# Splitting the first K load by partitions and the wq load by rows in a one-core decode kernel

## The chip, the cores and the metric

The kernel runs on one core of a Trainium2 chip. The metric is device time in microseconds (us); the time before is the median of three runs, 121.58 us (121.34 to 121.73). One further execution was taken with the hardware profiler; every profile line comes from that one. Its own time and its span are in the table further down.

The engines are named as in the profile: PE (matrix multiply), DVE (vector), ACT (scalar activations), POOL, and SP, which computes nothing here and issues nearly all DMA transfers. DMA work is done by 16 DMA engines that serve this core.

## The reference

Eight sequences each decode one token. A layer norm feeds two branches. Branch A is grouped-query attention over the last 1024 positions of a K/V cache; branch B is a gated feed-forward network. The result is the input plus A times silu of B.

```python
B, Sq, D = 8, 1, 512
Hq, Hkv, Sk, Dh = 32, 8, 4096, 128
W = min(4096, max(256, Sk // 4))                 # 1024
q = (x @ wq)                                     # wq: 512 x 4096
k = k_cache[:, :, Sk - W:, :]                    # 8 x 8 x 1024 x 128, bf16
v = v_cache[:, :, Sk - W:, :]
p = softmax(einsum(q, k) * Dh ** -0.5)
A = einsum(p, v) @ wo                            # wo: 4096 x 512
Bf = (gelu(x @ w_gate) * (x @ w_up)) @ w_down    # 512 x 1792, 512 x 1792, 1792 x 512
x = A_x; xn = layernorm(x)
return x + A(xn) * silu(Bf(xn))
```

Everything is bf16. The K and V windows are 16 MB each (8 sequences of 2 MB); wq and wo are 4 MB each; the three feed-forward matrices are 1.75 MB each.

## The kernel before

The program is written for one core, with the order of every engine's work fixed by the source (a manual schedule). Synchronisation is generated: each transfer from SP or ACT takes the next of eight DMA semaphores in turn, numbered 0 to 7, and a transfer also waits until the one that had the same semaphore before it, eight transfers earlier, has landed.

Loading. All big tiles live in a ring of eight slots of 128 partitions by 16 KB (`slot`, L62). `load_cache` (L69) loads one sequence's K or V as two transfers (g = 0 and 1), each of four heads: 128 partitions by 8 KB, 1 MB. On the DRAM side a transfer is 32 groups of positions by 4 heads, with 8 KB contiguous each; group p and head n go to partition 4p + n. The loads are issued by SP in this order: K of sequence 0 (L88), wq in two transfers of 2 MB (L93; 16 KB per partition, contiguous), K of sequence 1, V of sequence 0; then, inside the loop over sequences (L398), K two sequences ahead and V one ahead; then the feed-forward weights (L422, L425), and wo (L436), whose last megabyte goes in three pieces of 640, 256 and 128 KB. The token input x (8 partitions by 1 KB) is issued by ACT (L67) and has semaphore 0; the first K transfer has semaphore 1.

Computing. DVE turns each half K tile with one 32x32-block transpose (`turn_k`, L232). PE computes q from xn and wq, 32 matmuls of 512 columns, k outermost (L245 to L253), so that the first 8 need the first quarter of wq. For each sequence: scores (`scores`, L280), softmax (L303), turning of the probabilities (L326), values (L333), and a gather of the output (L354). At the end the two branches are finished, the last matmuls use the last wo piece (L498), and two DVE operations (L506, L508) make the output, which SP stores (L510).

The end of the program. After the store, SP waits on the eight DMA semaphores and the engines' own semaphores with one waiting instruction after another, in this order: semaphore 2; 3 and 1; 4 and 0; 5 and DVE's; 6 and PE's; 7 and ACT's; then POOL's. Then comes a barrier over all engines. Before the change the store is the 45th transfer, and has semaphore 4.

Of the kernel before, what the change touches and what calls it, by code (L numbers as in the profile page):

```python
# [21 lines left out]
def kernel(  # L22
# [13 lines left out]
    nc = tc.nc  # L36

    B, Sq, D = A_x.shape
    Hkv, Sk, Dh = A_k_cache.shape[1], A_k_cache.shape[2], A_k_cache.shape[3]
# [3 lines left out]
    win0 = Sk - W  # L43
    F = B_w_gate.shape[1]
    inv = float(Dh) ** -0.5
    P = nc.NUM_PARTITIONS
    NK = D // P
    HG = 4
    NG = Hkv // HG
    C = W * HG // P  # L50
# [11 lines left out]
    def slot(name):  # L62
        return ring.tile([P, 2 * ROW], BF16, name=name, tag="slot")
# [2 lines left out]
    x_sb = keep.tile([B, D], BF16, name="x_sb")  # L66
    nc.scalar.dma_start(out=x_sb, in_=A_x.flatten_outer_dims())  # L67

    def load_cache(cache, b, name):  # L69
        t = slot(name).rearrange("p (g x) -> p g x", g=NG)  # L70
        for g in range(NG):
            nc.sync.dma_start(  # L72
                out=t[:, g],
                in_=cache[b, g * HG : (g + 1) * HG, win0:Sk, :].rearrange(
                    "n (p c) d -> p n (c d)", c=C
                ),
            )
        return t

    k_sb, v_sb = {}, {}  # L80

    def load_k(b):
        k_sb[b] = load_cache(A_k_cache, b, "k_sb")

    def load_v(b):
        v_sb[b] = load_cache(A_v_cache, b, "v_sb")

    load_k(0)  # L88
    wq_v = A_wq.rearrange("(p k) n -> p k n", k=NK)
    wq_sb = []  # L90
    for i in range(2):
        t = slot("wq_sb").rearrange("p (k n) -> p k n", k=NK // 2)
        nc.sync.dma_start(out=t, in_=wq_v[:, i * (NK // 2) : (i + 1) * (NK // 2), :])  # L93
        wq_sb += [t[:, k, :] for k in range(NK // 2)]
    load_k(1)
    load_v(0)

# [4 lines left out]
        out=ident,  # L102
        in_=ident,
# [13 lines left out]
        out=xpad,  # L117
        in_=xpad,
# [17 lines left out]
        out=xhat,  # L136
# [9 lines left out]
    with tc.tile_pool(name="ps_x", bufs=1, space=PSUM) as ps_x:  # L146
# [26 lines left out]
        out=hv,  # L173
        in_=hv,
# [7 lines left out]
        out=neg_st,  # L182
        in_=neg_st,
# [8 lines left out]
        out=neg_mv,  # L192
        in_=neg_mv,
# [12 lines left out]
    for g in range(NG):  # L206
        nc.vector.tensor_reduce(
            out=sel[:, g, g * qd : (g + 1) * qd],
            in_=ident.rearrange("p (t g h) -> p g h t", t=4, g=NG)[:, g],
# [5 lines left out]
        out=own, in_=ident.rearrange("p (i e) -> p e i", e=8), axis=AX.X, op=ALU.add  # L215
    )
    pick = consts.tile([P, 4 * NU], BF16, name="pick")
    with nc.allow_low_precision(reason="sums of zeros and a single one"):
        nc.vector.tensor_reduce(
            out=pick, in_=ident.rearrange("p (a e) -> p a e", e=8), axis=AX.X, op=ALU.add  # L220
# [177 lines left out]
    for b in range(B):  # L398
        if b + 2 < B:
            load_k(b + 2)  # L400
        if b + 1 < B:
            load_v(b + 1)
            turn_k(b + 1, 0)
        softmax(b)
        if b + 1 < B:
            scores(b + 1, 0)
        if b >= 1:
            gather(b - 1)
        if b + 1 < B:
            turn_k(b + 1, 1)  # L410
            scores(b + 1, 1)
        turn_p(b)
        values(b)
        keep_o(b)
        if b == 4:
            regroup(0)
# [10 lines left out]
    for u in range(NU):  # L427
        if u % 2 == 0:
            pair = slot("wo_sb").rearrange("p (v j d) -> p v j d", v=2, d=D)
        t = pair[:, u % 2]  # L430
        src = A_wo[u * 1024 : (u + 1) * 1024, :].rearrange("(p j) d -> p j d", j=8)
# [14 lines left out]
    for n, ws in (("z_ps", wgu[0]), ("u_ps", wgu[1])):  # L446
# [15 lines left out]
        out=z2, in0=z2, scalar1=0.044715, scalar2=1.0, op0=ALU.mult, op1=ALU.add  # L462
# [11 lines left out]
        out=hT.rearrange("p j b -> p (j b)"), in_=h_bf.rearrange("p (y j) -> p j y", j=NJ)  # L474
    )
    f_ps = ps_f.tile([P, DT], FP32, name="f_ps")
    for j in range(NJ):
# [11 lines left out]
        out=g_sb, in0=g_sb, scalar1=0.5, scalar2=0.5, op0=ALU.mult, op1=ALU.add  # L489
# [5 lines left out]
    for u in range(NU):  # L495
# [15 lines left out]
        out=out_f.rearrange("b (t d) -> t b d", t=4), in_=out_sb[0 : P : RB, :]  # L511
# [31 lines left out]
```

## Time and profile before

| what | before |
|---|---|
| median of 3 runs | 121.58 us |
| profiled execution, own time | 121.8 us |
| its span | 119.7 us |
| bytes read | 47.46 MB |
| PE, DVE, ACT busy | 74.1, 75.8, 31.4 us |
| DMA mean over the span | 398 GB/s |
| first K transfer: issued, landed after | 0.81 us, 5.4 us |
| store issued | 116.84 us |

The profiled execution's own time is 2.1 us more than its span: that part lies around the span and no view shows it. The page gives the span in 40 slices of about 3 us, with the busy share of the DMA engines in tenths and the GB/s that they moved. A window table gives the same for stretches of any length: the engines' busy times, the granted clock of PE, the share of the 16 DMA engines and the GB/s. A share of 1.00 means that all sixteen were busy throughout. Records that straddle an edge of a window can make a share slightly over 1.

### The profile page before, as it was taken

The numbers are of one execution on the slowest core, as the hardware profiler recorded it, in microseconds if no ns is written. First come the engines' busy times: TensorE is split into PE (matmuls) and PEld (weight loads), VectorE is DVE, ScalarE is ACT, GpSimd is POOL, SyncE is SP. The second block draws the span as 40 slices with busy tenths as digits, with TensorE's granted clock in tenths as the row PEclk, the third lists the DMA queues.
The fourth block names the chain that finished last, engine by engine and source line by source line (L and its number), as shares of the span: only waits on it lengthen the run. The fifth ranks groups of instructions, "written<-read, shape, count | busy, mean of one in ns | idle before, by whom it ended". The sixth has DMA issues, their size and how long they took to land.

```text
span 119.7 us, 2300 instructions
## 1 busy us (share of the span) xinstructions
PE 74.1 (62%) x992; PEld 38.7 (32%) x992; DVE 75.8 (63%) x101; ACT 31.4 (26%) x75; POOL 3.2 (3%) x10
## 2 busy tenths in 40 slices
PE   0100499811994988969687684992994547535460
PEld 0100133300341544535443351450353433134340
DVE  3698820499739999999859959909943232651010
ACT  4600000676007151441612510700616110200000
POOL 2150000000000000000000000000000000000000
PEclk9999999985599999999999998599589755555555
DMA  2999999999999999999999999999999999999930
GB/s 66 394 457 433 411 416 427 430 433 422 427 427 433 419 419 427 435 411 430 430 433 405 430 430 430 411 430 435 424 419 447 422 451 412 434 403 430 402 118 3
DMA packets 6254, 47.61 MB, mean 398 GB/s; under 512 B 732, under 2 KB 868, under 8 KB 1124
## 3 DMA queue, kind: packets, MB, share of 16 engines
q1 hardware_dynamic: 6228, 47.46, 94.5%
q8 instruction: 8, 0.13, 0.4%
q10 hardware_dynamic: 16, 0.01, 0.0%
q14 instruction: 2, 0.02, 0.0%
HBM read 47.46 MB, written 0.01 MB: 397 GB/s over the span
## 4 chain that ended last, share of the span: by engine, by line
DMA 63%; PE 16%; DVE 14%; issue 2%; ACT 2%; SPq 1%; DVEq 0%
DMA wo_sb<-in_A_wo_dram 20%; DMA k_sb<-in_A_k_cache_dram 17%; DMA v_sb<-in_A_v_cache_dram 16%; DMA wq_sb<-in_A_wq_dram 9%; PE q_ps L247 8%; PE S_ps L295 6%; DVE kT L234 5%; DVE qbd L269 2%; DVE mx L305 2%; DVE q_both L260 1%; ACT P_sb L317 1%; PE s_ps L498 1%; DVE q_both L257 1%; SPq L72 1%; PE O_ps L339 1%
## 5 line engine op out<-in xcount | busy, mean ns | idle before, releaser
L295 PE MATMUL S_ps<-kT,qbd 128*128 128x512 bf16 x128 | 34.4, 416 | 14.9 <-DVE kT L234 11.5
L234 DVE STREAM_TRANSPOSE kT<-k_sb 128x2048 int32<-128x2048 int32 x16 | 36.5, 2289 | 4.6 <-DMA k_sb<-in_A_k_cache_dram 4.6
L295 PEld LDWEIGHTS <-qbd 128*128 128x128 bf16 x128 | 12.9, 103 | 32.4 <-issue 17.0
L247 PE MATMUL q_ps<-wq_sb,xnR 128*128 128x512 bf16 x32 | 9.8, 482 | 8.8 <-DMA wq_sb<-in_A_wq_dram 8.8
L315 ACT ACTIVATE nb<-m 32x1 f32<-32x1 f32 x32 | 6.4, 201 | 22.7 <-DVE m L312 22.4
L305 DVE TENSOR_REDUCE mx<-S_ps 128x1 f32<-128x1024 f32 x8 | 9.6, 1195 | 4.1 <-PE S_ps L295 4.1
L317 ACT ACTIVATE P_sb<-S_ps,nb 128x1024 bf16<-128x1024 f32 x8 | 11.1, 1391 | 0.3
L339 PE MATMUL O_ps<-v_sb,pT 128*32 128x128 bf16 x512 | 9.3, 228 | 2.6 <-DVE pT L328 2.6
L339 PEld LDWEIGHTS <-pT 128*32 128x32 bf16 x512 | 7.8, 101 | 5.6 <-issue 3.0
L352 ACT COPY O_sb<-O_ps 128x256 f32<-128x256 f32 x8 | 3.0, 372 | 23.5 <-PE O_ps L339 23.5
L247 PEld LDWEIGHTS <-xnR 128*128 128x128 bf16 x32 | 3.7, 118 | 14.6 <-issue 12.6
L328 DVE STREAM_TRANSPOSE pT<-P_sb 128x512 int32<-128x512 int32 x8 | 5.7, 711 | 3.4 <-ACT P_sb L317 2.8
L257 ACT CAST q_both<-q_ps 128x512 bf16<-128x512 f32 x6 | 3.0, 613 | 16.7 <-PE q_ps L247 16.7
L360 PE MATMUL o_ps<-O_sb,sel 128*32 128x128 f32 x32 | 6.1, 325 | 0.9 <-ACT O_sb L352 0.9
L498 PE MATMUL s_ps<-wo_sb,oT 128*32 128x128 bf16 x128 | 4.4, 307 | 3.4 <-DMA wo_sb<-in_A_wo_dram 3.3
L284 PE MATMUL S_ps<-neg_mv,neg_st 128*128 128x512 bf16 x16 | 4.8, 381 | 1.9 <-DVE q_both L257 1.9
L257 DVE CAST q_both<-q_ps 128x512 bf16<-128x512 f32 x2 | 1.3, 672 | 6.9 <-ACT q_both L257 6.9
L360 PEld LDWEIGHTS o_ps<-O_sb,sel 128*32 128x32 f32 x32 | 3.4, 128 | 5.0 <-issue 1.7
L498 PEld LDWEIGHTS <-oT 128*32 128x32 bf16 x128 | 3.5, 136 | 4.4 <-issue 4.2
L506 DVE TENSOR_TENSOR y<-s_ps,g_sb 128x128 f32<-128x128 f32 x1 | 0.3, 290 | 6.9 <-PE s_ps L498 6.9
L239 DVE MEMSET qbd<- 128x4096 uint32 x1 | 3.5, 3472 | 0.8 <-issue 0.8
L479 PE MATMUL f_ps<-wd_sb,hT 128*32 128x128 bf16 x56 | 1.7, 311 | 3.2 <-DVE hT L473 3.2
(64 smaller groups left out, 48.9 us busy)
## 6 DMA issues: line engine op xcount, KB each, us to landing
k_sb<-in_A_k_cache_dram SPq DMA_DIRECT2D x16, 1024.0 KB, 19.9
v_sb<-in_A_v_cache_dram SPq DMA_DIRECT2D x16, 1024.0 KB, 19.6
wq_sb<-in_A_wq_dram SPq DMA_DIRECT2D x2, 2048.0 KB, 11.3
wo_sb<-in_A_wo_dram SPq DMA_DIRECT2D x3, 1024.0 KB, 25.0
wgu_sb<-in_B_w_gate_dram SPq DMA_DIRECT2D x1, 1792.0 KB, 21.3
wgu_sb<-in_B_w_up_dram SPq DMA_DIRECT2D x1, 1792.0 KB
wd_sb<-in_B_w_down_dram SPq DMA_DIRECT2D x1, 1792.0 KB, 24.9
wo_sb<-in_A_wo_dram SPq DMA_DIRECT2D x1, 640.0 KB, 24.1
```

The source lines that it names most:

```text
L234: nc.vector.transpose(out=t.bitcast(I32), in_=k_sb[b][:, g].bitcast(I32))
L247: nc.tensor.matmul(q_ps[i], xnR[:, k, :, :].rearrange("p j b -> p (j b)"), wq_sb[k][:, i * 512 : (i + 1) * 512], start=(k == 0), stop=(k = ...
L257: e(out=q_bf[:, i * 512 : (i + 1) * 512], in_=q_ps[i])
L284: nc.tensor.matmul(S[b][:, half, :], neg_st.rearrange("p j h -> p (j h)"), neg_mv.rearrange("p a n -> p (a n)"), start=True, stop=False,)
L295: nc.tensor.matmul(S[b][:, half, :], qbd[:, m, b, w, g, :], kv[:, half * 16 : (half + 1) * 16, m, :, w], start=False, stop=(g == NG - 1 an ...
L305: nc.vector.tensor_reduce(out=mx, in_=S[b].rearrange("p a c -> p (a c)"), axis=AX.X, op=ALU.max)
L315: nc.scalar.mul(nb[32 * j : 32 * j + 32, :], m1, -inv)
L317: nc.scalar.activation(out=P_sb[b].rearrange("p c i w -> p c w i"), in_=S[b].rearrange("p a (c w i) -> p (a c) w i", w=2, i=32), func=ACT.Exp,
L328: nc.vector.transpose(out=pT[b].rearrange("p c h w -> p (c h w)").bitcast(I32), in_=P_sb[b].rearrange("p c i w -> p (c i w)").bitcast(I32),)
L339: nc.tensor.matmul(O_ps[b][32 * t : 32 * t + 32, g, :], pT[b][:, c // 2, :, c % 2], vv[:, c, :], start=(c < 4), stop=(c >= C - 4),)
L360: nc.tensor.matmul(o[:, 0:Dh], sel[:, g, :], O_sb[b][:, g, :], start=(g == 0), stop=(g == NG - 1))
L498: nc.tensor.matmul(s_ps[32 * t : 32 * t + 32, :], oT[:, j, u, :], wo[u][:, j, t * DT : (t + 1) * DT], start=(u == 0 and j == 0), stop=(u = ...
```

## The change

The first transfer (K of sequence 0, g = 0) becomes two of 64 partitions each: partitions 0 to 63, then 64 to 127. Each takes 16 of the 32 position groups, with 4 heads each; rows stay 8 KB. wq becomes four transfers of 1 MB, one for each k: 128 rows of 8 KB, which lie 32 KB apart in DRAM. The order of everything else stays. Three transfers are added, so all later transfers move on by three in the turn of the eight semaphores; x keeps semaphore 0, the halves have 1 and 2, K's second transfer 3, wq 4 to 7, and the store is the 48th and has semaphore 7. DVE's first transpose waits for both halves, and each group of eight q matmuls for its own wq transfer. No other engine's instructions change.

```diff
-    def load_cache(cache, b, name):
+    def load_cache(cache, b, name, parts=None):
         t = slot(name).rearrange("p (g x) -> p g x", g=NG)
         for g in range(NG):
-            nc.sync.dma_start(
-                out=t[:, g],
-                in_=cache[b, g * HG : (g + 1) * HG, win0:Sk, :].rearrange(
-                    "n (p c) d -> p n (c d)", c=C
-                ),
+            src = cache[b, g * HG : (g + 1) * HG, win0:Sk, :].rearrange(
+                "n (p c) d -> p n (c d)", c=C
             )
+            if parts is not None and g == 0:
+                parts(t[:, g], src)
+            else:
+                nc.sync.dma_start(out=t[:, g], in_=src)
         return t
 
     k_sb, v_sb = {}, {}
 
+    def first_load(dst, src):
+        for a, z in ((0, P // 2), (P // 2, P)):
+            nc.sync.dma_start(out=dst[a:z], in_=src[a // HG : z // HG])
+
     def load_k(b):
-        k_sb[b] = load_cache(A_k_cache, b, "k_sb")
+        k_sb[b] = load_cache(A_k_cache, b, "k_sb", first_load if b == 0 else None)
...
     for i in range(2):
         t = slot("wq_sb").rearrange("p (k n) -> p k n", k=NK // 2)
-        nc.sync.dma_start(out=t, in_=wq_v[:, i * (NK // 2) : (i + 1) * (NK // 2), :])
-        wq_sb += [t[:, k, :] for k in range(NK // 2)]
+        for k in range(NK // 2):
+            nc.sync.dma_start(out=t[:, k, :], in_=wq_v[:, i * (NK // 2) + k, :])
+            wq_sb.append(t[:, k, :])
```

## The prediction, made before the result was known

> **What bounds the kernel now.** I read the slices first, then windows over the span, the chain of waits, SP's own waits, and the two ends.
>
> The page's slices, busy share of the DMA engines and GB/s:
>
> ```profile
> DMA  2999999999999999999999999999999999999930
> GB/s 66 394 457 433 411 416 427 430 433 422 427 427 433 419 419 427 435 411 430 430 433 405 430 430 430 411 430 435 424 419 447 422 451 412 434 403 430 402 118 3
> ```
>
> The window table, cut where the first K row and the last weight row lie (columns: stretch, length, five engines' busy time, granted PE clock, DMA share, GB/s):
>
> ```profile
> 0.00:2.25 2.25, 0.00 (x0) 0.00 (x0) 0.39 (x3) 0.83 (x1) 0.78 (x7) 1.00 0.04 7
> 2.25:115.50 113.25, 73.50 (x980) 38.42 (x981) 74.83 (x96) 30.54 (x75) 2.38 (x3) 0.85 1.00 420
> 115.50:118.10 2.60, 0.65 (x16) 0.32 (x11) 0.58 (x2) 0.00 (x0) 0.00 (x0) 0.50 0.02 6
> ```
>
> From 2.25 to 115.50 us all sixteen DMA engines are busy: share 1.00. No engine comes near that (PE 73.5 of 113.25 us). So this is a kernel of three pieces: 2.25 us until the first row moves, 113.25 us of transfer, and 4.2 us from the last row to the end of the span. Time is saved or lost only where a piece changes; compute that starts earlier is worth nothing as long as the queue is full. Two more windows price the rows: one while mostly wq moves in 16 KB rows, one with K and V alone in 8 KB rows.
>
> ```profile
> 6.00:12.50 6.50, 0.00 (x0) 0.00 (x0) 5.64 (x7) 0.00 (x0) 1.78 (x2) 1.00 1.02 432
> 40.00:75.00 35.00, 27.51 (x442) 15.01 (x440) 31.05 (x32) 10.85 (x30) 0.00 (x0) 0.98 1.01 425
> ```
>
> The two ends: SP's issues from the timeline, then the close of the chain of waits, and what SP waits for after 115 us.
>
> ```profile
> 0.80 0.58 ACTq L67 DMA_DIRECT2D x_sb<-in_A_x_dram  x1
> 0.81 1.30 SPq L72 DMA_DIRECT2D k_sb<-in_A_k_cache_dram  x2
> 2.15 1.12 SPq L93 DMA_DIRECT2D wq_sb<-in_A_wq_dram  x2
> ...
> 3.31 1.20 SPq L72 DMA_DIRECT2D k_sb<-in_A_k_cache_dram  x2
> ...
> 4.55 1.29 SPq L72 DMA_DIRECT2D v_sb<-in_A_v_cache_dram  x2
> ```
>
> ```profile
> 90.71 24.12 DMA wo_sb<-in_A_wo_dram
> ...
> 116.52 0.29 DVE out_sb L508
> ```
>
> ```profile
> SPq L538 <- DMA out_dram<-out_sb: 1.0, 1, 1.0
> ```
>
> SP issues far ahead: the eight first big transfers are issued by 5.84 us, while the engines move 1 MB in 2.47 us (1,048,576 B at 425 GB/s). At the end the last weight row frees PE, DVE and the store, and SP then waits 1.0 us for the store alone.
>
> **The change, part by part.**
>
> *Three more issues on SP* (one K, two wq), about 0.6 us each: the second K issue took 0.58 us, and the two of wq 1.12 us together. K of sequence 1 is so issued near 5.1 us instead of 3.31. It is needed when the 6 MB ahead of it are through, at 2.25 + 6 x 2.47 = 17 us: the backlog covers it by 12 us. The first transfers behind the new queue also get earlier partners to wait for: V of sequence 0, second half, is issued at 5.24 us now and will wait for K's second transfer to land (about 9 to 11 us); it is needed at 2.25 + 9 x 2.47 = 24 us. Cost 0; were that cover gone, an issue and its start would cost about 1.4 us (0.81 to 2.25). DVE's first transpose gets one more wait and PE two; both are off the bound.
>
> *Four wq transfers of 8 KB rows.* 4,194,304 B take 9.71 us at 432 GB/s and 9.87 at 425: +0.16 us, if the difference of those windows is one of the row size. The trace's DMA packet records say the same: 309 ns for 8 KB, 611 for 16 KB, so 7 ns more per 16 KB, 16 times on each engine, +0.11; three more transfers add three completion writes of 9 ns per engine, +0.03. I take +0.15 us. Bounds: 0, and, since no row of the trace has an 8 KB row every 32 KB, the slowest page slice after the start, 402 GB/s: 10.43 us, +0.7. wo's 8 KB rows and K's, whose DRAM layouts differ, have the same 309 ns, so I stay by the low end. PE can start q after 1 MB instead of 2; nothing on the path comes of it.
>
> *The store on the last semaphore.* The instruction records show the wait that holds the store's semaphore (4) ending at 118.665 us, and the following waits of SP at 118.729, 118.790, 118.850 and 118.917. All of these wait for things long done and merely run in a row. With the store on semaphore 7 the first three are done before it lands: 118.917 - 118.729 = 0.19 us off the end. Nothing else is late there, because all other engines are already waiting at the barrier: -0.19 us, firm. Bounds -0.25 and -0.1.
>
> *The first K row earlier.* SP's first issue runs 0.81 to 1.47 us, and K's rows begin at 2.25, 0.78 us after its end. The 8-row x transfer begins 0.37 us after its issue (0.80 + 0.58 = 1.38; rows at 1.75). If that gap grows with the number of rows (0.41 us for 120 rows), 64 rows save 0.22 us; if it is of another kind, 0; if the second half, issued 0.66 us later, is late for some engines, a loss of 0.1. I take -0.10 us.
>
> *Two halves of 64 partitions: the uncertain term.* Work done by the engines is the same: 128 rows, 8 per engine, now 4 and 4. No big transfer of the trace writes fewer than 128 partitions, so I bound it. If a DMA engine's own pace is the limit (420 / 16 = 26 GB/s), a half takes 1.23 us, and the loss is 0. If the limit lies where the rows are written, 128 partitions take 425 GB/s, 3.3 GB/s each, and 64 take 212: 2.47 us per half, 4.93 for both, a loss of 2.47. What decides? Three DRAM layouts (K, wo, the feed-forward weights) reach the same pace, so the source doesn't set it; engines and destinations do, and these come together in every big row. The x transfer is the only row with few partitions: 61 and 21 GB/s in two slices of 0.1 us, so up to 7.6 GB/s for each of 8 partitions. It speaks for the engines, but at 1 KB per row it may never have filled a buffer. The half transfer is nearest to the full K transfer (same 8 KB rows, same 16 engines), so I take the destination's pace, less one row's time (0.31 us) for engines that begin the second half while neighbours still drain the first: +2.15 us, with 0 and +2.47 as ends.
>
> [...]
>
> *Sum.* 0 + 0.15 - 0.19 - 0.10 + 2.15 = +2.0 us. The profiled execution took 121.8 us (span 119.7 and 2.1 around it), so 123.8 there; it stands 0.2 us over the median of the runs, so against 121.58 I say **123.6 us**, 1.7% slower.
>
> **The rivals.**
>
> 1. *The engines' own pace is the limit, and the halves cost nothing.* 0 + 0.15 - 0.19 - 0.10 = -0.14: 121.45 us. For it: x's 7.6 GB/s per partition. Against it: nothing in the trace tells engines from destinations. With the start at its best (-0.22) and wq free, -0.41: 121.15, faster. This rival decides the sign once the halves cost under 0.14 us, that is once 64 partitions take over about 400 GB/s.
> 2. *Each half goes to only eight of the engines.* Then both halves run beside each other, eight rows per engine as before, but the eight engines of the second half start 0.66 us later, the second issue's distance, and end the kernel later. +0.66 - 0.10 + 0.15 - 0.19 = +0.5: 122.1 us. Against it: the trace's transfers of 128 rows all put 8 rows on each of 16 engines; nothing shows 64.
> 3. *wq is the slow part.* Rows 32 KB apart come at 402 GB/s: +0.7 in place of +0.15, with the halves free: 122.0 us. Nothing in the trace speaks for it.
>
> **How the numbers follow.** My forecast has 0.66 (its own range 122.6 to 124.2: half of the halves' cost at the low end, 2.47 and wq's upper part at the high end). Rival 1 has 0.25, split by the start term and the wq term: 0.12 faster than 0.3%, and 0.13 within it. Rival 2 has 0.06 and rival 3 0.03. 0.3% is 0.36 us, about what runs of this kernel can tell from no change: under 121.22 is faster, over 121.94 slower. Slower is 0.66 + 0.06 + 0.03, less 0.02 for cases that end inside the band: 0.73. The same is 0.15, faster 0.12. For 8 in 10, the range reaches from 124.2 down to 121.3, so that it takes in the middle of rival 1.
>
> **What would show each step.** In the profile after: the window from the first K row to 7 us should show about 210 GB/s while the first megabyte moves (DMA share still near 1, since slow rows count as busy), and K's halves land near 5 and 7.5 us instead of one transfer at 6.2; later slices stay at 425 GB/s, and everything from wq on lies 2 us later. If the first slices still show 400 GB/s and the last weight row ends at 115.4, rival 1 holds. Landings of the two halves only 0.66 us apart, with a low share, mean rival 2. wq windows under 420 GB/s mean rival 3. At the end, SP should wait for nothing between the store's landing and the barrier: the last wait starts about 0.2 us closer to the barrier. My forecast is wrong above all if a partition takes more than 3.3 GB/s.

## The result and the profile after

The changed kernel takes 122.97 us against 121.64 us in the same comparison: 1.0103 times as long, with a 95% interval of 1.0083 to 1.0122. It is slower by about 1.3 us. In 8 of the 20 executions of the four kernels that cut a K transfer into 64-partition halves, and in none of the others, the time was 3 to 5.5 us longer still (here one of six, 127.54 us); ratios leave these out, but medians and highest times hold them. The profiled execution took 122.98 us, with a span of 121.1 us (before: 121.8 and 119.7).

The page's slices after, busy share of the DMA engines and GB/s:

```profile
DMA  2999999999999999999999999999999999999940
GB/s 51 263 338 430 428 428 419 422 428 433 428 430 428 428 411 425 422 430 430 430 425 422 422 425 422 425 430 430 425 428 428 442 441 403 419 427 430 408 171 3
```

While the transfers run, only the second and third slices differ much from before (263 and 338 GB/s in place of 394 and 457; the others up to the 38th stay within 24 GB/s), though the engines are as busy there: digits of 9 all along. The windows of the start show it more finely; first before, then after (columns as in the prediction, the last two are DMA share and GB/s):

```profile
2.25:5.00 2.75, 0.52 (x8) 0.32 (x8) 1.78 (x8) 2.10 (x4) 0.00 (x0) 1.00 1.01 352
5.00:7.50 2.50, 0.00 (x0) 0.00 (x0) 2.33 (x11) 0.28 (x2) 2.10 (x3) 1.00 1.01 416
7.50:10.00 2.50, 0.00 (x0) 0.00 (x0) 2.50 (x2) 0.00 (x0) 0.28 (x1) 1.00 1.05 446
```

```profile
2.25:5.00 2.75, 0.51 (x8) 0.31 (x8) 1.75 (x8) 2.07 (x4) 0.00 (x0) 1.00 1.04 256
5.00:7.50 2.50, 0.00 (x0) 0.00 (x0) 2.02 (x10) 0.30 (x2) 2.07 (x3) 1.00 1.01 239
7.50:10.00 2.50, 0.00 (x0) 0.00 (x0) 2.14 (x1) 0.00 (x0) 0.31 (x1) 1.00 1.00 423
```

Until 7.5 us the engines move 239 to 256 GB/s with a share of 1: busy, but most rows take nearly twice as long (the fourth to the eighth of each engine 537 to 628 ns in the mean, before 312 to 369). From 7.5 us on the rate is back (423 GB/s). SP's issues after, and the time from issue to landing of the two halves:

```profile
0.80 1.32 SPq L85 DMA_DIRECT2D k_sb<-in_A_k_cache_dram  x2
2.17 0.60 SPq L78 DMA_DIRECT2D k_sb<-in_A_k_cache_dram  x1
2.81 2.03 SPq L99 DMA_DIRECT2D wq_sb<-in_A_wq_dram  x4
```

```profile
DMA to landing us min/median/max: 4.7/5.5/6.2
```

The second fence belongs to line 85, which issues the two halves: the first lands 4.7 us after its issue at 0.80 us, so at 5.5, the second 6.2 us after its own at 1.56, at 7.8. Before, the whole transfer landed 5.4 us after 0.81.

The three pieces of the span, from the records of its DMA rows and the span's end:

| piece | before | after | difference |
|---|---|---|---|
| start to the first K row | 2.25 us | 2.28 us | +0.03 |
| first K row to the end of the last weight row | 113.27 us | 114.87 us | +1.59 |
| last weight row to the end of the span | 4.14 us | 3.95 us | -0.19 |
| span | 119.66 us | 121.09 us | +1.43 |

SP's wait for the store's landing at the end is now

```profile
SPq L544 <- DMA out_dram<-out_sb: 0.8, 1, 0.8
```

0.8 us in place of 1.0: the wait is the same landing, seen by a later one of the waiting instructions.

### The profile page after: what moved, and what is told of

Same layout as the page of the kernel before. It is cut to its first block, busy times and chain, and to the rows that moved or that the text cites. A ratio compares the mean times of both kernels' runs of the same rounds, so it can differ in the third digit from the quotient of the medians.

```text
span 121.1 us, 2304 instructions
## 1 busy us (share of the span) xinstructions
PE 73.3 (61%) x992; PEld 37.9 (31%) x992; DVE 76.2 (63%) x101; ACT 31.4 (26%) x75; POOL 3.2 (3%) x10
## 4 chain that ended last, share of the span: by engine, by line
DMA 77%; PE 14%; DVE 3%; SPq 2%; issue 1%; DVEq 0%
DMA k_sb<-in_A_k_cache_dram 33%; DMA wo_sb<-in_A_wo_dram 20%; DMA v_sb<-in_A_v_cache_dram 16%; DMA wq_sb<-in_A_wq_dram 8%; PE q_ps L253 7%; PE S_ps L301 4%; DVE kT L240 2%; SPq L85 1%; PE s_ps L504 1%; PE O_ps L345 1%; PE o_ps L366 1%; DVE q_both L263 1%; SPq L78 1%; PE r_ps L394 0%; DVE y L512 0%
## 5 line engine op out<-in xcount | busy, mean ns | idle before, releaser
L345 PE MATMUL O_ps<-v_sb,pT 128*32 128x128 bf16 x512 | 8.7, 220 | 2.6 <-DVE pT L334 2.6
L345 PEld LDWEIGHTS <-pT 128*32 128x32 bf16 x512 | 7.2, 97 | 5.6 <-DVE pT L334 2.6
L275 DVE COPY qbd<-q_both 32x256 bf16<-32x256 bf16 x11 | 3.4, 358 | 0.0
```

What stands on the lines that cost most here:

```text
L345: nc.tensor.matmul(O_ps[b][32 * t : 32 * t + 32, g, :], pT[b][:, c // 2, :, c % 2], vv[:, c, :], start=(c < 4), stop=(c >= C - 4),)
```

## The experiments

Three explanations stood after this. **A:** the halves carry the loss, because rows written to partitions 0 to 63 alone, or 64 to 127 alone, take twice as long. **B:** part of it comes from the wq rows. **D:** it comes from more transfers at the start as such; with the narrower **C**, that the first transfer is cut in two, whichever way. Within A, what limits was open: each partition's own intake, as my forecast had it, so that any 64 partitions take rows of about 618 ns (P2), or something that goes with which 64 they are, so that 32 to 95 could keep the 309 ns of a whole transfer where 0 to 63 don't (P1). Row times below are means over 16 rows in the order of their starts, about one per DMA engine, from the trace's DMA packet records. The "moving stretch" is the second piece of the table above, from the first K row to the end of the last weight row; each is read from one trace.

### The halves alone

```diff
-        for k in range(NK // 2):
-            nc.sync.dma_start(out=t[:, k, :], in_=wq_v[:, i * (NK // 2) + k, :])
+        nc.sync.dma_start(out=t, in_=wq_v[:, i * (NK // 2) : (i + 1) * (NK // 2), :])
```

> The first K transfer in two halves of 64 partitions, wq in two transfers as before, so that the store has semaphore 5. Theory A (the halves carry the whole loss): the rows of the first megabyte take about twice as long, 618 in place of 309 ns, and the later slices run at 425 GB/s; the store saves one waiting step, 0.06 us. Span 1.4 to 1.6 us over before, time near 123.0 us, the same as with the whole change. Theory B (the 8 KB rows of wq, 32 KB apart, carry a third or more of the loss): span at most 1.0 us over before, time at most 122.6 us.

Measured: 1.0109 of before (1.0084 to 1.0135), as with the whole change. Span 121.5 us, 1.9 over before, more than the 1.4 to 1.6 expected. Its windows:

```profile
2.25:5.00 2.75, 0.52 (x8) 0.32 (x8) 1.65 (x7) 1.98 (x3) 0.00 (x0) 1.00 1.03 229
5.00:7.50 2.50, 0.00 (x0) 0.00 (x0) 2.12 (x11) 0.39 (x3) 1.97 (x3) 1.00 1.03 239
7.50:10.00 2.50, 0.00 (x0) 0.00 (x0) 1.93 (x1) 0.00 (x0) 0.41 (x1) 1.00 1.07 452
```

The slow first megabyte is there without the wq edit. The moving stretch is 115.12 us, +1.85. Its first row per engine takes 859 ns (716 with the change), its second to eighth 384, 471, 618, 584, 528, 615 and 621 ns, not 309. A holds, B falls.

### wq alone

```diff
     for i in range(2):
         t = slot("wq_sb").rearrange("p (k n) -> p k n", k=NK // 2)
-        nc.sync.dma_start(out=t, in_=wq_v[:, i * (NK // 2) : (i + 1) * (NK // 2), :])
-        wq_sb += [t[:, k, :] for k in range(NK // 2)]
+        for k in range(NK // 2):
+            nc.sync.dma_start(out=t[:, k, :], in_=wq_v[:, i * (NK // 2) + k, :])
+            wq_sb.append(t[:, k, :])
```

The rest is the kernel before, so the store has semaphore 6.

> wq in four transfers of 8 KB rows, the first K transfer whole, the store on semaphore 6. Theory A: 256 rows more at 7 ns each over 16 engines, and 32 completion writes, +0.13 us; two waiting steps less at the end, -0.12 us; time within 0.1 us of before, 121.6 us. Theory B: +0.4 us or more, 122.0 us, with wq rows longer than 309 ns.

Measured: 121.41 against 121.78 us, 0.9979 (0.997 to 0.9988): 0.2% faster than before, which I had not expected. Of wq's 512 rows 510 take 309 ns. In the profiled pair the span explains 0.06 us of it: moving 113.33 us (+0.05), end 4.03 us (-0.12). Over all executions on record the mean span is 0.10 us shorter (119.62 against 119.72) and the time around it 0.17 us (1.86 against 2.03). That second part lies where the profile shows nothing; it is not explained.

### The halves along the columns, twice

```diff
     def first_load(dst, src):
-        for a, z in ((0, P // 2), (P // 2, P)):
-            nc.sync.dma_start(out=dst[a:z], in_=src[a // HG : z // HG])
+        for a, z in ((0, ROW // 2), (ROW // 2, ROW)):
+            nc.sync.dma_start(out=dst[:, a:z], in_=src[:, :, a:z])
```

> The whole change, but the first K transfer is halved along the columns: two transfers of 128 partitions by 4 KB. Number of transfers, issues, waits and the store's semaphore (7) are those of the change. Theory A (what costs is that a transfer reaches 64 partitions only): 4 KB rows near 160 ns, first megabyte at the pace of before; +0.07 for 128 more rows, +0.14 for wq, -0.19 at the end: 121.6 us, within 0.15 us of before. Theory C (what costs is that the first transfer is cut in two, or the three added issues): 122.6 us or more, as with the change.

Measured: 122.41 us, 1.0053 (1.0033 to 1.0074): between the two theories. The first megabyte moves at nearly its old pace: most rows of 4 KB take 159 ns, and, with each row's bytes spread over its time, 1 MB has moved by 5.49 us against 5.36 before and 6.78 with the change. But this trace's first rows begin at 2.85 us, about 0.5 later than in any other, the last four rows of 4 KB end one after another until 6.85 us, and the first rows of K's second transfer take 363 to 395 ns. The moving stretch is 113.26 us, as long as before, so this trace's loss is the late start. The same kernel again, for a second trace:

> The halves by columns once more, for a second trace of the start. If a first transfer of 4 KB rows starts late by itself, its first rows begin near 2.85 us again, against 2.25 us in every other kernel, and the time is 122.0 us or more. If that start was an accident of one execution, they begin at 2.25 us and the time is 121.6 us.

Measured: 122.69 us, 1.0073 (1.005 to 1.0097). Here the first rows begin at 2.28 us, so the late start doesn't come each time; the kernel is slow all the same, and now the moving stretch holds it: 114.71 us, 1.44 over before. The windows of this second trace:

```profile
2.25:5.00 2.75, 0.51 (x8) 0.31 (x8) 1.91 (x9) 2.23 (x5) 0.00 (x0) 1.00 0.86 310
5.00:7.50 2.50, 0.00 (x0) 0.00 (x0) 1.86 (x9) 0.15 (x2) 2.23 (x3) 1.00 1.04 298
7.50:10.00 2.50, 0.00 (x0) 0.00 (x0) 2.34 (x2) 0.00 (x0) 0.15 (x1) 1.00 0.99 400
```

1 MB has moved by 5.65 us (rows of 4 KB take 159 to 229 ns in the mean), yet the next stretch drops to 298 GB/s: the first sixteen rows of the transfer behind the 4 KB rows take 309 to 1840 ns, 919 in the mean. What makes them slow is not settled. The time of this second run is what theory C said (122.6 us or more), so the times alone don't separate A from C for a first transfer. The row times do: this pair shows that the doubled rows of the first megabyte go with the 64 partitions; it doesn't show that a first transfer cut in two is otherwise free.

### K's second transfer by columns, the first whole

```diff
-            if parts is not None and g == 0:
+            if parts is not None and g == 1:
                 parts(t[:, g], src)
...
-        for a, z in ((0, P // 2), (P // 2, P)):
-            nc.sync.dma_start(out=dst[a:z], in_=src[a // HG : z // HG])
+        for a, z in ((0, ROW // 2), (ROW // 2, ROW)):
+            nc.sync.dma_start(out=dst[:, a:z], in_=src[:, :, a:z])
```

> As the run of halves by columns, but K's second transfer is cut (128 partitions by 4 KB twice), the first stays whole; wq in four, the store on semaphore 7. If the 0.6 us of that run belong to a first transfer of 4 KB rows, they are gone: 0.0 to 0.15 us under before, 121.6 us, first rows at 2.25 us. If they belong to rows of 4 KB wherever they are, the time stays near 122.4 us.

Measured: 121.48 against 121.76 us, 0.998 (0.9969 to 0.999). The number of transfers, the semaphores and the wq rows are those of the change; the only differences are which K transfer is cut, and in which direction. It is faster than both kernels, so D falls for cuts behind the first transfer: three more transfers cost nothing by themselves. The loss of the column halves belongs to their being first.

### Probes: which 64 partitions

One transfer of 64 partitions is put ahead of the kernel before, into a tile that nothing reads.

```diff
+    probe = keep.tile([P, ROW], BF16, name="probe")
+    src = A_k_cache[0, 0:HG, win0:Sk, :].rearrange("n (p c) d -> p n (c d)", c=C)
+    nc.sync.dma_start(out=probe[32:96], in_=src[32 // HG : 96 // HG])
     load_k(0)
```

and the same with 0 and 64 in place of 32 and 96.

> The kernel before with one more transfer ahead of all others: 64 partitions, numbers 32 to 95, of the first K rows (8 KB each, 0.5 MB) into a tile that nothing reads. 64 rows on 16 engines. [...] Theory P2 (each partition takes 3.3 GB/s, whichever it is, as the forecast had it): rows near 618 ns, +2.0 to 2.5 us. The store has semaphore 5, one waiting step less, -0.06 us. Time 122.8 us under P1, 123.6 to 124.0 us under P2.

> As the probe of partitions 32 to 95, with partitions 0 to 63: the same number of rows, bytes, engines and issues. P1: rows near 618 ns as in the change's halves, 0.7 to 1.2 us slower than the probe of 32 to 95. P2: the same time as that probe.

Measured: 122.97 us for 32 to 95 (1.0112, 1.0085 to 1.0139), 123.50 us for 0 to 63 (1.0152, 1.0121 to 1.0182). Windows of the start, first for 32 to 95, then for 0 to 63:

```profile
2.25:5.00 2.75, 0.51 (x8) 0.31 (x8) 1.81 (x8) 2.13 (x4) 0.00 (x0) 1.00 0.98 328
5.00:7.50 2.50, 0.00 (x0) 0.00 (x0) 2.14 (x11) 0.25 (x2) 2.13 (x3) 1.00 1.02 423
```

```profile
2.25:5.00 2.75, 0.51 (x8) 0.31 (x8) 1.80 (x8) 2.11 (x4) 0.00 (x0) 1.00 1.05 238
5.00:7.50 2.50, 0.00 (x0) 0.00 (x0) 1.98 (x10) 0.26 (x2) 2.12 (x3) 1.00 1.01 419
```

Each engine has four rows of the probe, if the 64 are shared evenly. For 32 to 95 they take 828 (the first row after the idle start), 350, 309 and 309 ns; for 0 to 63, 688, 432, 501 and 658, and the next transfer's first row 597. Same bytes, same count of partitions, same engines: P1 holds and P2 falls. 32 to 95, half from each side of the middle, keep the 309 ns of 128 partitions in their third and fourth rows. Four rows of 309 ns are 1.24 us on each engine; the moving stretch with 32 to 95 is 1.11 us longer than before. Nor is it the place in DRAM: of the position groups that this probe reads (8 to 23), the upper half belongs to the change's second half, whose rows take 537 to 628 ns in the mean. The moving stretches differ by 0.67 us (114.38 and 115.06), the medians by 0.53; I had said 0.7 to 1.2.

### Both K transfers of sequence 0 in halves

```diff
-            if parts is not None and g == 0:
+            if parts is not None:
```

> The whole change, with K's second transfer of sequence 0 in halves of 64 partitions as well (the store comes to semaphore 0, which saves nothing at the end). Theory A (each such half costs its rows' doubled time): the second megabyte is met by engines that run already, so all of its 8 rows per engine take near 618 ns: 2.3 us more than with the change plus 0.19 at the end, near 125.5 us, last weight row near 119.4 us. Theory D (the loss belongs to the start, where the first rows wait anyway, and not to the halves): within 0.4 us of the change, about 123.2 us.

Measured: 1.0285 (1.0255 to 1.0315, from two executions); the profiled execution took 125.33 us. The last weight row ends at 119.48 us, as expected. Windows:

```profile
5.00:7.50 2.50, 0.00 (x0) 0.00 (x0) 1.96 (x10) 0.25 (x2) 2.13 (x3) 1.00 1.06 239
7.50:10.00 2.50, 0.00 (x0) 0.00 (x0) 1.98 (x1) 0.00 (x0) 0.25 (x1) 1.00 1.01 220
10.00:12.50 2.50, 0.00 (x0) 0.00 (x0) 0.33 (x1) 0.00 (x0) 0.00 (x0) 1.00 0.99 252
```

The slow stretch is twice as long. The moving stretch is 117.20 us: the second megabyte costs 2.33 us more than the change's 114.87, close to the full 2.47, while the first cost about 1.5 (1.59 less wq's share). So part of the price is hidden when the halves come first, and D falls once more. Set beside the run before the probes: this second transfer cost 2.33 us cut by partitions and nothing cut by columns.

### The second half from ACT's queue

```diff
-        for a, z in ((0, P // 2), (P // 2, P)):
-            nc.sync.dma_start(out=dst[a:z], in_=src[a // HG : z // HG])
+        for e, a, z in ((nc.sync, 0, P // 2), (nc.scalar, P // 2, P)):
+            e.dma_start(out=dst[a:z], in_=src[a // HG : z // HG])
```

> The whole change, but ACT issues the second half (partitions 64 to 127) right after x, while SP issues the first: both halves in flight together on two queues. Theory A with the two queues served in turn by each engine: partitions 0 to 63 and 64 to 127 are written at the same time, rows fall back towards 309 ns, the first megabyte moves at 350 GB/s or more, 121.6 to 121.9 us. Theory S (the halves are served one after the other all the same): rows near 618 ns, 122.8 us or more.

Measured: the four executions took 122.94, 125.95, 128.39 and 128.47 us; none is near the 121.6 to 121.9 of theory A. The trace is that of the longest, so only its start is read here, and no ratio is given:

```profile
2.25:5.00 2.75, 0.52 (x8) 0.32 (x8) 1.70 (x7) 2.71 (x3) 0.00 (x0) 1.00 1.03 262
5.00:7.50 2.50, 0.00 (x0) 0.00 (x0) 2.08 (x11) 0.35 (x2) 2.02 (x3) 1.00 1.02 262
```

ACT issues its half at 1.45 us; its rows begin only at 4.21 us, when SP's half is nearly through (its last rows end at 4.9), and SP's next rows at 6.39, when ACT's are nearly through. Of ACT's 64 rows 43 take 598 to 615 ns and the others 374 to 564; the rate is 262 GB/s. Theory S: the halves were served one after the other although they were on two queues.

### x in two transfers and wq in four; x in four alone

```diff
-    nc.scalar.dma_start(out=x_sb, in_=A_x.flatten_outer_dims())
+    for r in range(0, B, B // 2):
+        nc.scalar.dma_start(out=x_sb[r : r + B // 2], in_=A_x.flatten_outer_dims()[r : r + B // 2])
```

with wq in four as above; the second kernel has `B // 4` and the wq of before. Both bring the store to semaphore 7 without touching K.

> No halves of K. wq in four transfers, and x in two of 4 rows each on ACT's queue: three more transfers as in the change, the store on semaphore 7, and no transfer of big rows reaches fewer than 128 partitions. Theory A: -0.19 at the end, +0.05 for wq's rows as in the run of wq alone: 0.14 to 0.2 us under the kernel before measured beside it, about 121.55 us, faster than both kernels. Theory D (more transfers cost by themselves at the start): 122.0 us or more.

> The kernel before with x in four transfers of two rows each on ACT's queue; K and wq untouched. Only the store's semaphore changes (4 to 7) and 48 short completion writes are added. Theory A: SP's waits after the store are three fewer, the end after the last weight row 0.19 us shorter (4.14 to 3.95), time 0.15 to 0.2 us under before, 121.55 us. Theory B (the gain of the runs with wq in four comes from wq): no change, or more than 0.05 us slower.

Measured: 121.50 against 121.76 us, 0.9988 (0.9978 to 0.9998), for the first; 121.54 against 121.56 us, 0.9999 (0.9987 to 1.0011), for the second. The step that I meant to isolate is in the traces: from the store's issue to the end of SP's waits it takes 2.08 us with semaphore 4, 2.01 with 5, 1.94 with 6, and 1.88 to 1.90 with 7, about 0.06 us per waiting instruction. In the second kernel's trace 0.10 us of it went to a later last row (115.62 against 115.52) and 0.09 to a later store after that row (1.41 against 1.32), and the span is what it was. Over all executions on record its mean span is 0.14 us shorter than that of the kernel before (119.50 against 119.64), about what the step should give, but the time around the span is 0.11 us longer (2.03 against 1.92). So a gain of the semaphore by itself is not shown as time. The kernels with wq in four and no first transfer cut gain 0.1 to 0.2% (0.15 to 0.26 us), more than their mean spans do (0.04 to 0.12 us).

## Why the prediction was right or wrong

The direction, the place and the way the time is lost (rows of a half that take about twice as long at full DMA share) were right: 123.6 us forecast, 122.97 measured, +1.33 us in place of +2.0. The halves land at 5.5 and 7.8 us, near the forecast 5 and 7.5; the windows' 239 to 256 GB/s are above the forecast of about 210. The term for the halves was 0.6 us too large, the one for the first row had the wrong sign, and the reason given for the halves was wrong. As the traces show them, the terms 0 + 0.05 - 0.19 + 0.03 + 1.54 make the span's +1.43 us; the runs' +1.33 is 0.1 less. The profiled executions differ the same way in the part around the span that no view shows: 1.9 us after, 2.1 before.

- **Three more issues cost 0.** Right: DMA share stays at 1 throughout (1.00 from 2.25 to 117.00 us), and the kernel with K's second transfer by columns has as many issues and is faster than before.
- **wq, +0.15 us.** Nearly: +0.05 in the moving stretch of the run of wq alone, rows at 309 ns as the packet records said. That is no more than single traces differ by: x in four, with wq untouched, has +0.08. The bound of 0.7 us and rival 3 were far off; the run of wq alone came out 0.2% faster than before.
- **The store on the last semaphore, -0.19 us.** Right in the trace, to the hundredth (4.14 to 3.95 us).
- **The first row earlier, -0.10 us.** Wrong. With 64 rows the issue ends at 1.50 us and the first row begins at 2.28, a gap of 0.78 us (0.78 and 0.84 in the two probes), as before with 128 rows (0.78). Half the rows don't shorten the gap; extrapolating from the 8-row x transfer was the error. Why x has 0.37 us on ACT's queue stays open. The start became 0.03 us later, since the first issue took 0.69 instead of 0.66 us.
- **The two halves, +2.15 us.** The term that was mis-sized: 1.59 less wq's 0.05, so 1.54 us, in the changed kernel; 1.85 in the run of the halves alone. Before, the eight rows of the first megabyte take 707, 315, 340, 334, 314, 312, 369 and 333 ns per engine; after, 716, 405, 360, 587, 592, 537, 614 and 628, and then 596 and 358 for the next transfer. I took off one row's time for the change from first to second half. What I left out is at the start: the first row takes about 710 ns in either case, and the two after it run at 405 and 360. Why these two are faster than the ones behind them is not shown. Both K transfers in halves show the price without that start: 2.33 us for a megabyte.
- **The reason I gave for it, 3.3 GB/s per partition, was wrong,** and that the number came out near is luck: both P1 and P2 give rows of about 618 ns for partitions 0 to 63, and only another choice of 64 partitions tells them apart. The probes show that 32 to 95 take rows at 309 ns: in these runs the count of partitions doesn't set the pace, which partitions they are does. What it is in 0 to 63, or in 64 to 127, that sets it is not shown. The windows' 239 to 256 GB/s hold the faster rows of the start; the window from 7.50 to 10.00 us of the run with both transfers in halves has 220. A second queue changed little (262 GB/s, one half's rows behind the other's).
- **Rival 1** (the engines' own pace, halves free; its best case adds up to 121.17 us, not 121.15) falls by the windows of 239 to 256 GB/s, and **rival 2** (each half on eight engines) by the share of 1.01 to 1.04 and halves that land 2.3 us apart, not 0.66.

## What to carry to other kernels

When the DMA engines are busy from the first row to the last, a transfer's price is read from the rate while it moves, not from its issue: cutting a load into partition halves 0 to 63 and 64 to 127 cost 1.5 to 2.3 us per megabyte here, at full DMA share, where a cut along the columns of the second transfer cost nothing. A busy share of 1 doesn't say that the engines move at their pace (here 1.01 and 1.04 at 239 and 256 GB/s, where the same windows had 416 and 352 before); look at GB/s beside it. A fixed latency in front of a transfer should be tested for what it depends on before a change is built on it: half the rows did not shorten it by anything here (0.78 us with 64 rows and with 128). And a reason that gives the right number in one case should be tried where it and its rival differ, as 32 to 95 does here.

## What the runs showed of the hardware

- 64 partitions numbered 32 to 95 took 8 KB rows at 309 ns in the third and fourth row, as 128 do; 0 to 63 took these at 501 and 658 ns, and both halves of a transfer met by engines already at work took rows at 537 to 631 (means over sixteen rows).
- In transfers to 128 partitions a row takes close to 8.6 ns plus its bytes at 27.2 GB/s, a line fitted to the rows of these traces: 46, 84, 159, 196, 309, 535 and 611 ns for 1, 2, 4, 5, 8, 14 and 16 KB. Cutting wq's 16 KB rows in two cost 0.05 us for 4 MB, in one trace.
- The slow rate of a half was not undone by a second queue (262 GB/s): its rows began when the other queue's were nearly through.
- A first transfer of 4 KB rows went with slow first rows of the transfer behind it: 919 ns in the mean of the first sixteen in one trace, 384 in the other, and 309 where the same 4 KB rows came behind an 8 KB first transfer. Left open.
